# Blockwise attention followed by a channel mix: batches 0 and 1 keep token order in scores, exponentials and value products, and only the sums read the exponentials class by class

## The chip, the core and the metric

One Trainium2 chip, one core of it. The metric is the device time of one execution in microseconds (us). The kernel before took 270.37 us, the median of five executions (268.53 to 272.26). Differences under about one per cent are smaller than the spread of these five.

## What is computed

Two functions follow one another: an attention over 8 batches, 8 heads, 576 tokens and 64 dimensions, with a causal mask by blocks of 64 tokens, and a channel mix over the 4608 tokens by 512 channels that it gives.

```python
scores = scale * np.matmul(q, k.transpose(0, 1, 3, 2))
...
mask = block_i >= block_j
scores = np.where(mask, scores, -1000000000.0)
scores = scores - np.max(scores, axis=-1, keepdims=True)
attn = np.exp(scores)
attn = attn / (np.sum(attn, axis=-1, keepdims=True) + 1e-09)
return np.matmul(attn, v).astype(np.float32)
...
xk = mu_k * x + (1.0 - mu_k) * x_prev
xr = mu_r * x + (1.0 - mu_r) * x_prev
k = np.maximum(xk @ w_k, 0.0)
v = k * k @ w_v
r = 1.0 / (1.0 + np.exp(-(xr @ w_r)))
return (r * v).astype(np.float32)
```

All inputs are float32; the kernel works in bf16 and f16 for the matmul operands and adds up in float32. It takes no maximum before the exponential.

## The kernel before

**Attention.** For a batch, queries and keys of a pair of heads stand in `qkt` as 64 rows a head (the dimension) by 576 tokens. Batches 0 and 1 (`TURNED = 2`, line 21) get there by transposes on TensorE (`add_turned`, line 444) and lie in the order of the tokens. The six later batches are loaded so that one partition holds four tokens running, are transposed by a DMA (`add_qk`, line 509), and their first 512 tokens lie by class: first all tokens whose number is 0 modulo 4, then those with 1, and so on, 128 of each.

A **score** task (`add_score`, line 630; named s, batch, pair, number) multiplies a tile of 128 keys with a stretch of queries, for the two heads of a pair at once: each head uses 64 of the array's rows, and their two matmuls run side by side. Three such tasks cover a pair, and a fourth for each half batch the last 64 tokens (s, batch, t, half). Line 666 is the matmul over the first 512 tokens: a pair streams 1280 columns through it (batch 0: 384, 512 and 384 in its three tasks; the others: 512, 384 and 384), the two heads side by side. It writes PSUM by class for every batch. In the later batches a class is a run of neighbours. In batches 0 and 1 it is every fourth token, so the streamed operand is read with a step of four bf16 elements (8 bytes).

ScalarE takes the exponential of a task's scores in one instruction into `t_e` in f16 (line 695), and VectorE or GpSimd zeroes the masked corner of a diagonal tile (`zero`, line 702).

A **sum** group (`group` and `sums`, lines 747 to 808; tasks d and e) adds the exponentials over the keys. Its stationary operand is 32 columns of `FOURTH`, one of every four of which is one; class by class, a round of four matmuls, one for each of four heads, runs side by side in four groups of 32 array columns. So the sum of class j lands in partition j modulo 4, and 128 columns of PSUM hold 512 tokens. VectorE takes the reciprocal (line 796) and spreads each class over the partitions with a shuffle (line 805): `t_rd` holds the reciprocals by class. A half batch has 1280 columns of class sums for each of the four heads in batches 1 to 7; in batch 0 they are split into a group d with 384 and a group e with 896.

A **value** task (`part` and `value`, lines 762 and 810; tasks v) multiplies the exponentials with the values, again in four column groups, into PSUM by class. VectorE multiplies this with the reciprocals (`norm`, lines 841, 852 and 854) and writes `t_xt` in token order. In that product both inputs are read by class, with a step, and the output runs on.

**Channel mix.** It works on chunks of 512 tokens, the first one in two halves: the difference to the token before (line 930), two scaled additions (line 944), then TensorE tasks k (line 968), r (line 1007) and p (line 1038), with relu, square, tanh and the last product between them on ScalarE, VectorE and GpSimd.

**Order.** Nothing runs in the order in which the program text names it. `Plan` (line 92) holds every task with its engine, a planned duration, what it depends on and which ring of buffers it takes from. TensorE goes through the list `TENSOR` (line 24) exactly; `WHERE` (line 49) names an engine for each task that may run on more than one. The other engines' queues, SP's with the loads among them, and GpSimd's, follow from due times that the plan works out from the TensorE list and the planned durations. `FILL` tasks (line 1073) are dummy matmuls of 128 columns that the plan puts where TensorE would wait before its first k task.

Of the kernel before, what the change touches and what calls it, by code (L numbers as in the profile page):

```python
# [21 lines left out]


TENSOR = """
q000 q010 q001 q011 s0t0 s000 s010 q021 q031 q030 q020 s012 s030 d00 s0t1 s020
s002 q100 v000 s032 d01 q110 q101 q111 v010 s011 s001 s022 s021 e00 s031 k00
k02 k01 k03 v002 v001 s100 q121 e01 s110 s112 s102 q130 v012 v011 s111 s101
q131 q120 k07 k05 k04 k15 s1t0 s120 s1t1 k16 k10 k11 k14 k12 d10 s130 s132 k06
v101 s131 v100 r00 s121 s122 r10 k17 k13 v102 r11 s200 r01 s202 d11 v110 v111
p00 p01 s201 p10 s2t0 s210 p11 s212 k20 k21 k25 k23 k22 r22 s211 k27 r20 v112  # L30
d20 k24 k26 r23 v200 v201 r21 v202 s220 s222 p21 s221 s230 p20 s231 s232 p23
s2t1 s300 v211 d21 s301 v210 s302 p22 s320 s322 v212 s321 s330 s331 k30 k33
s3t1 s332 r32 k31 s310 s3t0 d31 k35 s312 s311 r30 k36 k34 d30 k32 k37 r31 v300
v311 v302 r33 v312 v301 v310 s400 s401 p30 p31 s402 s4t0 p32 s410 s412 p33
s430 k40 s432 k44 k41 s420 s411 k47 r41 s421 k43 s4t1 k45 s431 s422 d40 r42
k42 k46 r40 r43 v400 v402 d41 v401 v411 v410 s500 s501 p42 p41 v412 s5t0 s510
p43 s530 s511 p40 s502 s512 k50 k53 k56 k54 r53 s531 s532 d50 k52 r52 k55 s520
s522 k51 k57 r51 v502 v500 s5t1 s521 r50 p53 v501 d51 v512 v511 s600 s602 p52
v510 s601 s6t0 p50 s630 s632 p51 s610 s611 k60 k67 k62 s612 s620 r63 r61 k66
r62 s6t1 s622 k64 k65 d60 s621 s631 k63 k61 r60 v600 v601 d61 v602 p60 p62  # L40
s700 s702 v612 v610 v611 s701 p61 s720 s721 p63 s710 s722 k70 k73 s711 s712
k74 k72 s7t0 r73 s730 s7t1 d70 v700 r71 r72 s731 s732 k71 k75 k77 k76 v701 d71
v702 v711 p73 p71 v710 v712 p72 p70 r70 k80 k82 k81 k85 k87 k86 k84 k83 r80
r81 r83 r82 p82 p80 p81 r90 p83 r91 k90 k94 k97 k93 k92 k91 k95 k96 r93 r92
p90 p91 p92 p93b p93a
"""


WHERE = {
    "ACT": "ev001 ev011 ev030 ev100 ev110 ev120 ev131 qk1011 qk1100 qk1101 "  # L50
            "qk1110 qk1111 qk201 qk300 qk310 qk330 qk331 qk401 qk411 qk421 "
            "qk501 qk530 qk531 qk600 qk601 qk621 qk630 re02 re04 re06 re07 re11 "
            "re12 re15 re17 re20 re23 re24 re26 re27 re30 re31 re32 re33 re34 "
            "re35 re40 re43 re44 re46 re50 re51 re54 re57 re61 re63 re64 re66 "
            "re67 re70 re77 re80 re81 re82 re83 re85 re90 re91 re92 re95 re96 "
            "sq02 sq04 sq07 sq11 sq12 sq17 sq20 sq21 sq26 sq27 sq30 sq32 sq34 "
            "sq36 sq40 sq44 sq46 sq50 sq54 sq55 sq57 sq61 sq62 sq63 sq70 sq73 "
            "sq74 sq75 sq76 sq81 sq83 sq85 sq87 sq93 sq96 v02 v04 v11 v12 v14 "
            "v20 v21 v24 v30 v31 v40 v54 v70 wk0 wk1 wk2 wk4 wk5 wr1 wr2 wv0 "
            "wv1 wv2 wv3",  # L60
    "DVE": "d11 d12 d13 d21 d31 d33 d43 d52 d60 d62 d72 d82 d90 d91 d93 ev000 "
            "ev010 ev020 ev021 ev031 ev101 ev111 ev121 ev130 qk0010 qk0101 "
            "qk0110 qk1010 qk211 qk220 qk221 qk231 qk301 qk410 qk431 qk631 "
            "qk700 qk710 qk711 qk720 qk721 re00 re01 re03 re05 re10 re13 re14 "
            "re16 re21 re22 re25 re36 re37 re41 re42 re45 re47 re52 re53 re55 "
            "re56 re60 re62 re65 re71 re72 re73 re74 re75 re76 re84 re86 re87 "
            "re93 re94 re97 sq00 sq03 sq05 sq25 sq31 sq35 sq42 sq45 sq47 sq51 "
            "sq52 sq60 sq64 sq66 sq67 sq71 sq72 sq84 sq92 sq94 sq95 v22 v32 v33 "
            "v34 v42 v44 v50 v52 v60 v71 v72 wk6 wr0 wr3 wv4 wv5 wv6 wv7 z002 "
            "z020 z032 z100 z102 z112 z130 z200 z202 z221 z222 z230 z300 z301 "  # L70
            "z310 z321 z322 z330 z411 z412 z420 z421 z422 z430 z431 z432 z501 "
            "z502 z510 z511 z512 z520 z521 z522 z532 z602 z610 z620 z622 z630 "
            "z631 z632 z710 z730 z731",
    "POOL": "d00 d01 d02 d03 d10 d20 d22 d23 d30 d32 d40 d41 d42 d50 d51 d53 "
            "d61 d63 d70 d71 d73 d80 d81 d83 d92 qk0000 qk0001 qk0011 qk0100 "
            "qk0111 qk1000 qk1001 qk200 qk210 qk230 qk311 qk320 qk321 qk400 "
            "qk420 qk430 qk500 qk510 qk511 qk520 qk521 qk610 qk611 qk620 qk701 "
            "qk730 qk731 sq01 sq06 sq10 sq13 sq14 sq15 sq16 sq22 sq23 sq24 sq33 "
            "sq37 sq41 sq43 sq53 sq56 sq65 sq77 sq80 sq82 sq86 sq90 sq91 sq97 "
            "v00 v01 v03 v10 v13 v23 v41 v43 v51 v53 v61 v62 v63 v64 v73 v74 "  # L80
            "wk3 wk7 z000 z010 z012 z022 z030 z101 z110 z111 z120 z121 z122 "
            "z131 z132 z201 z210 z211 z212 z220 z231 z232 z302 z311 z312 z320 "
            "z331 z332 z400 z401 z402 z410 z500 z530 z531 z600 z601 z611 z612 "
            "z621 z700 z701 z702 z711 z712 z720 z721 z722 z732",
}


# [207 lines left out]
def kernel(  # L295
# [23 lines left out]
    J = 4  # L319
# [246 lines left out]
    def add_v(b):  # L566
        for sc in range(5):
            n = P if sc < 4 else D
            vl = plan.buf("vl")
            t = load(("vl", b, sc), lambda: new("vl", [P, H, D], FP),  # L570
                     lambda d, n=n, sc=sc: [(
                         d[0:n], v[b, :, sc * P:sc * P + n].rearrange(
                             "h p d -> p h d"))],
                     0.0051 * n, 0.0108 * n, takes=[vl])

            def fn(eng, n=n, sc=sc):
                convert(eng, VOs[b % 2][0:n, sc],
                        tiles["vl", b, sc][0:n])
            cast["v", b, sc] = flex(
                f"v{b}{sc}", {"POOL": 0.57, "DVE": 0.38, "ACT": 0.52},  # L580
                fn, [t] + ([cast["v", b - 1, 0]] if b and not sc else []),
                takes=[] if sc else [vo_buf[b]],
                uses=[vl] + ([vo_buf[b]] if sc else []))
# [46 lines left out]
    def add_score(b, pr, i):  # L630
# [23 lines left out]
        def fn():  # L654
# [4 lines left out]
            for p, col, kc, a, z in mms:  # L659
                for h in range(2):  # L660
# [1 line left out]
                    keys, ask = qkt[rows, p, 1], qkt[rows, p, 0]  # L662
                    w = z - a
                    keys = keys[:, kc * P:kc * P + P]
                    if a < M:
                        nc.tensor.matmul(  # L666
                            PS[:, h, col:col + J * w].rearrange(
                                "p (j n) -> p j n", j=J), keys,
                            ask[:, 0:CUT].rearrange(
                                "d (p j) -> d j p" if b < TURNED else  # L670
                                "d (j p) -> d j p", j=J)[:, :, a:z],
                            start=True, stop=True)
                    else:
# [28 lines left out]
        def zero(eng):  # L702
            for col, kc, a, z in pieces(b)[i]:
                if a == kc * 32 and a < M:
                    (nc.vector if eng == "DVE" else nc.gpsimd).memset(  # L705
                        tiles["e", b, pr][D:P, :, i, col:col + J * (
                            z - a)].rearrange(
                            "p h (j n) -> p h j n", j=J)[:, :, :, 0:D // J],
                        0.0)
# [3 lines left out]
                f"z{b}{pr}{i}", {"POOL": 0.19 * n, "DVE": 0.09 * n}, zero, [t],  # L713
                uses=[ebuf], lock=())

    def probs(b, head, kc, a, z):


        if kc == J:
# [5 lines left out]
        E = tiles["e", b, pr][:, h, i, col:]  # L725
        if a == M:
            return E[:, 0:D]
        return E[:, 0:J * (z0 - a0)].rearrange("p (j n) -> p j n", j=J)[
            :, :, a - a0:z - a0]

    def add_values(b, Q):

# [29 lines left out]
        def part(PS, xs, a, z):  # L762
            V = VOs[b % 2]
            wide = J * (z - a) if a < M else D
            for n, x in enumerate(xs):
                cols = slice(n * wide, n * wide + wide)
                kcs = [kc for kc in range(J) if kc * 32 < z] + [J] * (a == M)
                for kc in kcs:
                    lo = max(a, kc * 32)
                    for g in range(G):  # L770
                        ps = PS[:, cols]
                        if a < M:
                            ps = ps.rearrange("q (j n) -> q j n", j=J)[
                                :, :, lo - a:z - a]
                        tiled(ps, V[:, kc, 4 * Q + g, x:D:2],
                              probs(b, 4 * Q + g, kc, lo, z), g,
                              kc == kcs[0], kc == kcs[-1])

        def group(name, a, z, deps, steps, dur, r_dur, s_dur):
# [50 lines left out]
        def scale(t, i, xs, a, z, c, first, lo, hi, buf, rd, spr, key):  # L830
# [5 lines left out]
            def norm():  # L836
# [3 lines left out]
                if a == M:  # L840
# [4 lines left out]
                    return  # L845
                p0, p1 = (lo - b * S) // J, (hi - b * S) // J
                num = num[:, 0:n * J * (z - a)].rearrange(
                    "q (s j p) -> q s p j", s=n, j=J)[:, :, p0 - a:p1 - a]
                r = r[:, 0:J * MP].rearrange("q (j p) -> q p j", j=J)[:, p0:p1]
                x = x.rearrange("q s (p j) -> q s p j", j=J)  # L850
# [12 lines left out]
                xt_of[c].setdefault(2 * Q + x, []).append(n)  # L863

        if b == 0:
            rd = group(f"d0{Q}", 0, H2, after(0), 32, 0.34, 0.5, 0.56)
            value(0, (0, 1), 0, H2, after(0), 16, 0.34, *rd)
            rd = group(f"e0{Q}", H2, M, after(0, 1, 2), 84, 0.75, 0.9, 0.56)
            value(1, (0, 1), H2, M, after(1, 2), 32, 0.78, *rd)
        else:  # L870
            rd = group(f"d{b}{Q}", 0, M, after(0, 1, 2), 84, 0.84, 1.3, 0.82)
            value(0, (0,), 0, M, after(0, 1, 2), 16, 0.56, *rd)
            value(1, (1,), 0, M, after(0, 1, 2), 16, 0.56, *rd)
        value(2, (0, 1), M, WD, after(0, 1, 2) + [ready["l", b, Q]], 40, 0.34,
# [274 lines left out]
```

## Time and profile before

| what | value |
|---|---|
| median of five executions | 270.37 us (268.53 to 272.26) |
| the profiled execution, its own time | 271.18 us |
| span from its first to its last instruction | 269.4 us |
| TensorE matmul busy | 250.6 us, 93%, 4116 matmuls |
| VectorE busy | 228.6 us, 85% |
| ScalarE busy | 183.3 us, 68% |
| GpSimd busy | 108.8 us, 40% |
| DMA | 51.51 MB, mean 191 GB/s |

Each engine has its own row in the profile, with the time in which any of its instructions ran. A matmul's duration includes its way through the array, so matmuls overlap and the row says how much of the time at least one was under way. PE is TensorE, PEld its loads of the stationary operand, DVE VectorE, ACT ScalarE, POOL GpSimd, SP the engine that issues the transfers. In a group line, names stand as written<-read; shapes are partitions by elements.

### The profile page before, as it was taken

The numbers are of one execution on the slowest core, as the hardware profiler recorded it, in microseconds if no ns is written. First come the engines' busy times: TensorE is split into PE (matmuls) and PEld (weight loads), VectorE is DVE, ScalarE is ACT, GpSimd is POOL, SyncE is SP. The second block draws the span as 40 slices with busy tenths as digits, with TensorE's granted clock in tenths as the row PEclk, the third lists the DMA queues.
The fourth block names the chain that finished last, engine by engine and source line by source line (L and its number), as shares of the span: only waits on it lengthen the run. The fifth ranks groups of instructions, "written<-read, shape, count | busy, mean of one in ns | idle before, by whom it ended". The sixth has DMA issues, their size and how long they took to land.

```text
span 269.4 us, 9934 instructions
## 1 busy us (share of the span) xinstructions
PE 250.6 (93%) x4116; PEld 130.1 (48%) x4116; DVE 228.6 (85%) x577; ACT 183.3 (68%) x279; POOL 108.8 (40%) x213
## 2 busy tenths in 40 slices
PE   0798978999998979999999999999999999999995
PEld 0665656454453534544355454544554554444443
DVE  2469989989988696999689998999999999998533
ACT  1479979995767898937983789379736970471250
POOL 3555405634534242554457062236384143340310
PEclk9999979999999989999999999999999999999999
DMA  7999998999999999999999999999999101202204
GB/s 219 299 274 236 299 215 269 199 227 220 235 247 205 185 199 217 289 194 230 225 270 192 202 223 284 143 187 266 259 201 198 59 4 68 93 0 79 80 0 156
DMA packets 118301, 51.51 MB, mean 191 GB/s; under 512 B 102768, under 2 KB 109168, under 8 KB 118256
## 3 DMA queue, kind: packets, MB, share of 16 engines
q1 hardware_dynamic: 118256, 50.88, 86.0%
q8 instruction: 32, 0.52, 0.9%
q14 instruction: 13, 0.11, 0.1%
HBM read 33.56 MB, written 9.44 MB: 160 GB/s over the span
## 4 chain that ended last, share of the span: by engine, by line
PE 72%; DVE 12%; DMA 6%; ACT 6%; issue 2%; POOL 1%; SPq 1%; DVEq 0%; ACTq 0%; POOLq 0%
PE t_mm L968 20%; PE t_mm L1038 18%; PE t_mm L744 11%; PE t_mm L1007 10%; PE t_s L666 7%; ACT t_e L695 4%; DMA t_ld<-in_q_dram 4%; DMA t_qkt<-NB 2%; PE t_s L674 2%; PE t_mm L484 2%; DVE t_xt L852 2%; PE t_mm L1076 1%; DVE t_rd L805 1%; DVE t_k L992 1%; DVE t_o L1050 1%
## 5 line engine op out<-in xcount | busy, mean ns | idle before, releaser
L695 ACT ACTIVATE t_e<-t_s 128x1024 f16<-128x1024 f32 x96 | 94.9, 1027 | 26.9 <-PE t_s L666 15.2
L968 PE MATMUL t_mm<-t_xk,WK 128*128 128x512 f16 (+1 forms) x320 | 69.6, 365 | 0.1
L1038 PE MATMUL t_mm<-WV,t_k 128*128 128x512 f16 (+1 forms) x296 | 66.5, 374 | 0.0
L968 PEld LDWEIGHTS <-WK 128*128 128x128 f16 x320 | 29.7, 99 | 30.1 <-issue 2.9
L1038 PEld LDWEIGHTS <-t_k 128*128 128x128 f16 x296 | 27.2, 98 | 31.3 <-issue 2.0
L992 POOL TENSOR_TENSOR t_k<-t_kr 128x512 f16<-128x512 f32 (+1 forms) x24 | 23.4, 981 | 44.5 <-ACT t_kr L981 25.6
L930 POOL TENSOR_TENSOR t_d<-t_xt 128x512 f32<-128x512 f32 (+1 forms) x25 | 25.9, 1038 | 31.6 <-DVE t_xt L852 26.6
L666 PE MATMUL t_s<-t_qkt 64*128 64x128 bf16 (+3 forms) x272 | 35.1, 327 | 3.6 <-ACT t_e L695 3.2
L1018 ACT ACTIVATE t_t<-t_mm 128x512 f32<-128x512 f32 x36 | 21.4, 602 | 22.6 <-PE t_mm L1007 22.5
L1007 PE MATMUL t_mm<-WR,t_xr 128*128 128x512 f16 x144 | 35.9, 380 | 0.0
L705 POOL MEMSET t_e<- 64x128 f16 x65 | 12.5, 209 | 50.3 <-ACT t_e L695 45.3
L852 DVE TENSOR_TENSOR t_xt<-t_mm,t_rd 128x448 f32<-128x448 f32 (+6 forms) x56 | 30.6, 595 | 1.3 <-PE t_mm L744 1.2
L1050 DVE SCALAR_TENSOR_TENSOR t_o<-t_t,t_mm 128x512 f32<-128x512 f32 (+1 forms) x37 | 24.3, 666 | 8.5 <-PE t_mm L1038 8.3
L981 ACT ACTIVATE t_kr<-t_mm 128x512 f32<-128x512 f32 (+1 forms) x44 | 24.5, 563 | 8.1 <-PE t_mm L968 7.1
L744 PE MATMUL t_mm<-t_e,VO 128*32 128x64 f16 (+4 forms) x1056 | 29.2, 251 | 0.6 <-DVE t_kr L983 0.5
L944 DVE SCALAR_TENSOR_TENSOR t_xk<-t_d,MUK,t_xt 128x512 f16<-128x512 f32 (+1 forms) x40 | 28.9, 748 | 0.2
L944 DVE SCALAR_TENSOR_TENSOR t_xr<-t_d,MUR,t_xt 128x512 f16<-128x512 f32 (+1 forms) x40 | 28.4, 735 | 0.0
L674 PE MATMUL t_s<-t_qkt 64*128 64x64 bf16 x320 | 24.4, 198 | 2.4 <-ACT t_e L695 1.6
L983 DVE TENSOR_SCALAR t_kr<-t_mm 128x512 f32<-128x512 f32 (+1 forms) x36 | 21.9, 623 | 4.0 <-PE t_mm L968 3.8
L744 PEld LDWEIGHTS <-VO 128*32 128x32 f16 x1184 | 19.1, 97 | 12.4 <-issue 7.2
L990 ACT ACTIVATE t_k<-t_kr 128x512 f16<-128x512 f32 (+1 forms) x35 | 20.7, 601 | 2.0 <-DVE t_kr L983 1.5
L674 PEld LDWEIGHTS <-t_qkt 64*128 64x128 bf16 x320 | 14.5, 98 | 14.8 <-issue 11.6
(61 smaller groups left out, 289.7 us busy)
## 6 DMA issues: line engine op xcount, KB each, us to landing
out_dram<-t_o SPq DMA_DIRECT2D x35, 256.0 KB, 3.8
t_vl<-in_v_dram SPq DMA_DIRECT2D x32, 256.0 KB, 5.1
t_ld<-in_k_dram SPq DMA_DIRECT2D x48, 128.0 KB, 4.1
t_ld<-in_q_dram SPq DMA_DIRECT2D x24, 256.0 KB, 4.1
t_ld<-in_q_dram SPq DMA_DIRECT2D x8, 288.0 KB, 5.9
t_ld<-in_k_dram SPq DMA_DIRECT2D x8, 288.0 KB, 4.5
t_ld<-in_moe_w_k_dram SPq DMA_DIRECT2D x8, 256.0 KB, 4.9
t_ld<-in_moe_w_v_dram SPq DMA_DIRECT2D x8, 256.0 KB, 4.2
```

The costliest lines, as they stand in the source:

```text
L666: nc.tensor.matmul(PS[:, h, col:col + J * w].rearrange("p (j n) -> p j n", j=J), keys, ask[:, 0:CUT].rearrange("d (p j) -> d j p" if b < T ...
L674: nc.tensor.matmul(PS[:, h, col:col + D], keys, ask[:, CUT:S], start=True, stop=True)
L695: nc.scalar.activation(tiles["e", b, pr][:, :, i, 0:used], tiles["ps", b, pr, i][:, :, 0:used], AF.Exp, scale=ISQ)
L744: nc.tensor.matmul(ps[g * R:g * R + R], lhs, e, start=start, stop=stop, tile_position=(0, g * R))
L852: nc.vector.tensor_tensor(x[:, 0], num[:, 0], r, ALU.mult)
L930: e.tensor_tensor(d[:, 0:w], x[:, cc, o + 1:o + w + 1], x[:, cc, o:o + w], ALU.subtract)
L944: nc.vector.scalar_tensor_tensor(tiles[name, h][:, cc, o:o + w], tiles["d", c, cc][:, 0:w], (MUK1, MUR1)[n][:, cc:cc + 1], xt_tile(c)[:, c ...
L968: nc.tensor.matmul(ps[:, 0:w], WK[:, cc, jc * P:(jc + 1) * P], tiles["xk", h][:, cc, o:o + w], start=(cc == 0), stop=(cc == CCn - 1))
L992: (nc.vector if eng == "DVE" else nc.gpsimd).tensor_tensor(K2, KR, KR, ALU.mult)
L1007: nc.tensor.matmul(ps, tiles["xr", h][:, cc, o + jt * P:o + (jt + 1) * P], WR[:, cc], start=(cc == 0), stop=(cc == CCn - 1))
L1038: nc.tensor.matmul(ps[:, 0:w], tiles["k2", h][:, jc, off:off + P], WV[:, jc, cols], start=(jc == 0), stop=(jc == JCn - 1))
L1050: nc.vector.scalar_tensor_tensor(tiles["o", c, jt, part][:, 0:w], tiles["t", c, jt][:, cols], 1.0, tiles["pv", c, jt, part][:, 0:w], ALU.a ...
```

## The change

In batches 0 and 1 queries stay in token order. The score matmul streams `ask[:, J*a:J*z]`, a run of neighbours, and writes PSUM in the same order. The exponential is unchanged, and its result is then in token order. The masked corner is one run of 64 columns in place of 16 columns in each of four classes. The value products read the exponentials as one run and write PSUM as one run. The sums go on class by class, and so they now read every fourth f16 element of the exponentials (8 bytes apart). The product with the reciprocals reads PSUM as one run; the reciprocals it still reads by class. Batches 2 to 7 keep their code.

Four planned durations change: those of the sum groups of batches 0 and 1, and that of one conversion of values on VectorE. With them `TENSOR` and `WHERE` are replaced by a new order and a new assignment for the whole kernel; neither is shown here in full. TensorE issues the same matmuls less six of the dummies. Counted over the whole program, VectorE has 3 conversions of w_v and 6 relus fewer, and 5 squares and 2 differences more; ScalarE 6 conversions for q and k more and 8 squares of 512 fewer; GpSimd 3 conversions of w_v, 3 of w_r and 5 squares of 512 more, and 5 conversions for q and k fewer.

```diff
 TENSOR = """
-q000 q010 q001 q011 s0t0 s000 s010 q021 q031 q030 q020 s012 s030 d00 s0t1 s020
-s002 q100 v000 s032 d01 q110 q101 q111 v010 s011 s001 s022 s021 e00 s031 k00
+q000 q010 q011 q001 q020 q030 s000 s010 q021 s002 s012 q031 s030 s032 v000 d00
+q110 s020 q100 s011 s0t0 s001 d01 s021 s031 v010 e00 s0t1 s022 q111 q101 v002
...
             cast["v", b, sc] = flex(
-                f"v{b}{sc}", {"POOL": 0.57, "DVE": 0.38, "ACT": 0.52},
+                f"v{b}{sc}", {"POOL": 0.57, "DVE": 0.38 if sc < 4 else 1.0,
+                              "ACT": 0.52},
...
-                    if a < M:
+                    if a < M and b < TURNED:
+                        nc.tensor.matmul(PS[:, h, col:col + J * w], keys,
+                                         ask[:, J * a:J * z], start=True,
+                                         stop=True)
+                    elif a < M:
                         nc.tensor.matmul(
                             PS[:, h, col:col + J * w].rearrange(
                                 "p (j n) -> p j n", j=J), keys,
                             ask[:, 0:CUT].rearrange(
-                                "d (p j) -> d j p" if b < TURNED else
                                 "d (j p) -> d j p", j=J)[:, :, a:z],
                             start=True, stop=True)
...
                     (nc.vector if eng == "DVE" else nc.gpsimd).memset(
+                        tiles["e", b, pr][D:P, :, i, col:col + D]
+                        if b < TURNED else
                         tiles["e", b, pr][D:P, :, i, col:col + J * (
...
-    def probs(b, head, kc, a, z):
+    def probs(b, head, kc, a, z, flat=False):
...
-        return E[:, 0:J * (z0 - a0)].rearrange("p (j n) -> p j n", j=J)[
-            :, :, a - a0:z - a0]
+        E = E[:, 0:J * (z0 - a0)]
+        if b < TURNED and flat:
+            return E[:, J * (a - a0):J * (z - a0)]
+        return E.rearrange("p (n j) -> p j n" if b < TURNED else
+                           "p (j n) -> p j n", j=J)[:, :, a - a0:z - a0]
...
-                        if a < M:
+                        if a < M and b < TURNED:
+                            ps = ps[:, J * (lo - a):J * (z - a)]
+                        elif a < M:
                             ps = ps.rearrange("q (j n) -> q j n", j=J)[
                                 :, :, lo - a:z - a]
                         tiled(ps, V[:, kc, 4 * Q + g, x:D:2],
-                              probs(b, 4 * Q + g, kc, lo, z), g,
+                              probs(b, 4 * Q + g, kc, lo, z, True), g,
...
                 num = num[:, 0:n * J * (z - a)].rearrange(
+                    "q (s p j) -> q s p j" if b < TURNED else
                     "q (s j p) -> q s p j", s=n, j=J)[:, :, p0 - a:p1 - a]
...
-            rd = group(f"d0{Q}", 0, H2, after(0), 32, 0.34, 0.5, 0.56)
+            rd = group(f"d0{Q}", 0, H2, after(0), 32, 0.48, 0.5, 0.56)
-            rd = group(f"e0{Q}", H2, M, after(0, 1, 2), 84, 0.75, 0.9, 0.56)
+            rd = group(f"e0{Q}", H2, M, after(0, 1, 2), 84, 1.08, 0.9, 0.56)
-            rd = group(f"d{b}{Q}", 0, M, after(0, 1, 2), 84, 0.84, 1.3, 0.82)
+            rd = group(f"d{b}{Q}", 0, M, after(0, 1, 2), 84,
+                       1.2 if b < TURNED else 0.84, 1.3, 0.82)
```

## The prediction

> **What bounds the kernel now.** I read the page first: PE is under way in 93% of the span, and the chain that ended last runs through PE for 72% of it, with 7% in the score matmuls (L666) and 11% in sums and values (L744).
>
> ```profile
> span 269.4 us, 9934 instructions
> PE 250.6 (93%) x4116; PEld 130.1 (48%) x4116; DVE 228.6 (85%) x577; ACT 183.3 (68%) x279; POOL 108.8 (40%) x213
> PE 72%; DVE 12%; DMA 6%; ACT 6%; issue 2%; POOL 1%; SPq 1%; DVEq 0%; ACTq 0%; POOLq 0%
> ```
>
> Batches 0 and 1 are at work up to about 60 us, so I then asked for each engine's busy time by stretch (columns: busy us and count of PE, PEld, DVE, ACT, POOL, then granted clock, DMA share, GB/s).
>
> ```profile
> 20.00:33.70 13.70, 12.24 (x390) 7.91 (x389) 13.36 (x42) 13.54 (x21) 6.63 (x12) 1.00 1.00 268
> 33.70:37.10 3.40, 1.54 (x65) 1.09 (x68) 2.96 (x15) 3.40 (x5) 0.31 (x2) 1.00 0.86 202
> 37.10:40.50 3.40, 3.40 (x69) 2.48 (x57) 2.90 (x7) 1.64 (x4) 0.00 (x0) 0.50 0.95 228
> 45.00:60.00 15.00, 15.00 (x356) 8.35 (x355) 13.66 (x35) 15.00 (x29) 8.78 (x19) 1.00 1.10 212
> 140.00:235.00 95.00, 94.07 (x1670) 47.33 (x1669) 92.47 (x231) 60.70 (x88) 40.03 (x75) 1.00 0.86 172
> ```
>
> The reader is to see three stages. From 20 to 37 us ACT is full (16.94 of 17.10 us) and PE is not (13.78). From 45 us PE is full. From 140 us DVE, 92.47 of 95, is nearly as full as PE. Of PE's waits from 20 to 62 us, 2.2 us were for ACT, 1.2 for nothing that the profile shows, 0.5 for DVE:
>
> ```profile
> PE t_s L666 <- ACT t_e L695: 2.2, 4, 0.7
> PE t_mm L484 <- issue: 1.2, 1, 1.2
> PE t_mm L744 <- DVE t_kr L983: 0.5, 1, 0.5
> ```
>
> **A, the scores read a run.** The same matmuls exist in both forms. First group: 43 to 54.5 us, batch 1, step of four. Second: from 62 us, later batches, a run.
>
> ```profile
> L666 PE MATMUL t_s<-t_qkt 64*128 64x512 bf16 x4 | 1.2, 607 | 0.7 <-ACT t_e L695 0.7
> L666 PE MATMUL t_s<-t_qkt 64*128 64x256 bf16 x4 | 0.8, 394 | 0.0
> ...
> L666 PE MATMUL t_s<-t_qkt 64*128 64x512 bf16 x46 | 8.9, 384 | 0.9 <-ACT t_e L695 0.5 <-DMA t_qkt<-NB 0.4
> L666 PE MATMUL t_s<-t_qkt 64*128 64x256 bf16 x46 | 6.3, 273 | 0.5 <-ACT t_e L695 0.5
> ```
>
> The gain is 607-384 = 223 ns for 512 columns and 394-273 = 121 for 256, about 0.44 ns a column; with the step a column costs (607-394)/256 = 0.83 ns. The eight pairs stream 8 x 1280 = 10,240 columns, which would be 4.5 us. Not all of it counts. Before 20 us the array is slow, whatever the clock row shows: the 256-column value matmul, which reads a run, takes 407 ns there against 273 to 275 later, and the score with its step takes 394, as it does later.
>
> ```profile
> L666 PE MATMUL t_s<-t_qkt 64*128 64x256 bf16 x12 | 2.5, 394 | 0.0
> L744 PE MATMUL t_mm<-t_e,VO 128*32 128x256 f16 x8 | 0.7, 407 | 0.0
> ```
>
> So a score gains nothing there: seven tasks with 7 x 384 = 2688 columns. The two tasks of 384 in the stretch at clock 0.50 gain nothing either. Left are 10,240-2688-768 = 6784 columns by 0.44 = **3.0 us** of PE time.
>
> The Trainium skill's "SBUF — State Buffer", section "Door 1", holds that a step is free while a 16-byte line is hit twice, up to 8 bf16 elements. By that rule A and B would both be 0; the rows show 607 against 384 ns at a step of four, so the measurement decides, and I use it.
>
> **B, the sums read with a step.** No row has a column-tiled matmul reading with a step. In a run, the sum rounds of one half batch show in the timeline as these (start, length):
>
> ```profile
> 20.59 0.39 PE L744 MATMUL t_mm<-t_e,FOURTH 128*32 128x64 f16 x32
> 25.34 0.68 PE L744 MATMUL t_mm<-t_e,FOURTH 128*32 128x64 f16 x64
> 46.09 0.79 PE L744 MATMUL t_mm<-t_e,FOURTH 128*32 128x128 f16 x64
> ```
>
> Less about 0.18 for the last matmul's way out (the 32-column row has 179 ns) these are 0.21, 0.50 and 0.61 us for 384, 896 and 1280 columns in each of four heads. Lower end: 0, if four streams side by side hide the step. Upper end: the four streams of a round take turns, 4 x 0.83 = 3.32 ns a column; two half batches of d1 and e0 and one d0 after 20 us have 2560+1792+384 = 4736 columns, 15.7 us against 1.22+1.00+0.21 = 2.43 now, so 13.3. The nearest row is the score: its two streams run side by side, each at 0.83. I take that for four: 1280 x 0.83 = 1.06 (+0.45 each), 896 x 0.83 = 0.74 (+0.24 each), 384 x 0.83 = 0.32 (+0.11), together **+1.5 us**; the other d0 falls before 20 us.
>
> **What of A and B is on the path.** From 45 to 60 us PE is the bound; there lie five scores, 512+4x384 = 2048 columns, -0.9 us, and both d1 groups, +0.9: nothing. From 20 to 45 us it is -(6784-2048) x 0.44 = -2.1 and +0.6, net -1.5, but ACT sets the pace there, with exponentials of 1.03 us each that a faster score does not shorten; PE would wait longer for ACT in place of computing. Ends: 0 and -1.5. I take a third, **-0.5**, since a score also lies ahead of its own exponential.
>
> **C, the product with the reciprocals.** It reads PSUM as a run, the reciprocals with the step. With both stepped 512 elements take 1052 ns (L854); with both in runs 128 take 276 (L841) where the stepped 128 take 364. Per product of 512 the gain lies between 0 and 4 x 88 = 352 ns; eight products' worth, at most 2.8 us of DVE. Off the path to 45 us, where ACT decides: 0, at best -0.7.
>
> **D, the masked corner** is the same number of zeros in one run: 112 ns on DVE, 209 on POOL now; 0, hidden by POOL's 45.3 us of waiting for ACT before it. The removed dummies (six matmuls) ran only where PE waited: 0.
>
> **E, the new order.** Every queue is drawn anew, so each has steps moved past others. By counts times the rows' means DVE stays within 0.1 us, ACT loses 1.0, and POOL gains 2 to 4 (of that the three w_v conversions, which POOL does not show now, lie between its f16 cast, 608 ns, and its product of 512, 1119). POOL is busy 40%, which covers this on average. On SP the third and fourth loads are now both queries, so the first group's second key load comes one load (0.29 MB, at 230 to 284 GB/s some 1.1 us) later; ACT stands idle 4.2 of 12.6 us from 7.4 to 20 us, which covers it. If that cover is gone, +1.1. What the new order does to PE's 8.3 us of gaps after its start (269.4-250.6, less 7.4 before the first and 3.1 after the last matmul) and to the two stretches of 3.4 us at clock 0.50 (at 37.1 and 98.5 us, each worth up to 1.7) can't be read from this trace. I take 0, between -3 and +4.3 (below).
>
> **Sum.** 269.4-0.5+0+0+0 = 268.9 us of span; with the profiled execution's 1.8 us around it (271.18-269.4) 270.7. That execution is 0.8 above the median of the five, so **269.9** stands against 270.37: no change.
>
> **Rivals.**
> *All of it counts* (faster). The -1.5 is kept whole, and with fewer waits before it the stretch at clock 0.50 at 37 us does not come. For it: PE idled 1.86 of the 3.40 us ahead of that stretch. Against: most of that was 1.2 us of "issue", which the change does not touch. 269.9-1.0-1.7 = 267.2.
> *The new order puts in a stall* (slower). From 80 to 100 us the present order has one: PE is busy 17.39 of 20 us, waits for loads of queries, and then runs 3.4 us at half clock: 2.6+1.7 = 4.3. Another such gives 274.2; it decides above 2.7. For it: the DMA share is 0.86 to 1.3 to past 200 us, and DVE and POOL, which free the load buffers, have changed work. Against: the total work is the same.
> *The four streams take turns* (slower). Then B is up to 13.3 in place of 1.5, and 269.9+11.8 = 281.7; it passes one per cent once B exceeds 1.5+3.2 = 4.7 us, that is (4.7+2.43)/4736 = 1.5 ns a column. Against: two streams show 0.83, and four streams of runs show no turns (1280 columns in 0.61 us).
>
> **How the numbers follow.** A measurement of this kernel tells about one per cent from no change: 267.7 to 273.1. The forecast has 0.50; the faster rival 0.20; the stall 0.23; the turns 0.07. So faster 0.20, same 0.50, slower 0.30. The range takes in the faster rival and the stall with little beyond them, 266.5 to 274.5, and leaves out the turns; for the forecast alone, the ends of A and B's net with C give 268.2 to 270.4, and with half of E's 4.3 above and the one per cent below its own range is 267.7 to 272.5.
>
> **What would show it.** A: the score matmul of 512 columns in batch 1 at about 384 ns. B: the x64 rounds with FOURTH in batch 1 at about 1.25 us in place of 0.79; 0.8 would mean a free step, over 2 turns. The path: PE's wait for ACT before the scores, 2.2 us now, grows if I am right that ACT sets the pace. C: the product of 512 elements in batch 0 below 1052 ns. E: the stretches at clock 0.50, two now, and PE's gaps from 60 to 210 us. The prediction is wrong if those gaps or stretches change by more than the whole of A and B.

## The result and the profile after

| | before | after |
|---|---|---|
| median | 270.27 us (48 runs, 267.56 to 273.63) | 272.72 us (27 runs, 269.59 to 277.46) |
| ratio, 95% interval | | 1.0080 (1.0057 to 1.0104) |
| profiled execution, its span | 271.18, 269.4 us | 272.81, 271.0 us |

The kernel became 0.8% slower, 0.0080 x 270.3 = 2.2 us, with 1.5 to 2.8 us as the interval. The ratio compares the fast runs of the two, those at most 1.5% above the fastest run of their kernel, so it is not the quotient of the two medians. The time lies inside the range of the prediction, but the forecast had summed to -0.5 us, and the interval leaves that out. In what follows, line numbers are those of each kernel: a line of the sums is L744 before, L753 after, L752 or L751 in some experiments.

The page of after, with busy time, clock row and the chain that ended last:

```profile
span 271.0 us, 9939 instructions
...
PE 249.0 (92%) x4110; PEld 132.2 (49%) x4110; DVE 229.5 (85%) x576; ACT 182.8 (67%) x279; POOL 116.8 (43%) x214
...
PEclk9999979999999999999999999999999999999999
...
PE 56%; DVE 19%; DMA 12%; ACT 6%; issue 3%; SPq 2%; POOL 2%; DVEq 0%; POOLq 0%; ACTq 0%
```

PE is under way 1.6 us less than before (249.0 against 250.6), and yet the span is 1.6 us longer. So PE stands still for longer. The chain says the same: PE carries 56% of it in place of 72%, and what PE waits for, DVE and DMA, went from 12% and 6% to 19% and 12%. The same stretches as before, with the columns as before:

```profile
20.00:33.70 13.70, 10.68 (x368) 7.59 (x367) 13.37 (x40) 10.85 (x19) 8.78 (x17) 1.00 0.89 234
...
37.30:40.71 3.41, 3.41 (x52) 2.53 (x45) 3.14 (x7) 3.41 (x6) 1.29 (x3) 0.51 1.16 250
45.00:60.00 15.00, 13.41 (x343) 8.77 (x345) 10.69 (x32) 14.18 (x30) 9.20 (x13) 1.00 1.22 241
60.00:80.00 20.00, 18.58 (x233) 8.75 (x225) 19.05 (x54) 11.94 (x20) 6.27 (x10) 1.00 1.08 233
80.00:100.00 20.00, 18.99 (x344) 9.41 (x343) 18.56 (x45) 16.24 (x21) 10.90 (x20) 1.00 1.15 193
100.00:120.00 20.00, 19.09 (x404) 9.59 (x402) 16.52 (x49) 14.51 (x24) 7.21 (x14) 1.00 1.16 245
```

The kernel before, in the stretches that the prediction did not show:

```profile
60.00:80.00 20.00, 20.00 (x256) 9.06 (x254) 18.50 (x47) 14.04 (x22) 9.01 (x16) 1.00 1.03 226
80.00:100.00 20.00, 17.39 (x313) 8.56 (x312) 16.37 (x40) 16.49 (x21) 8.33 (x19) 0.96 1.20 200
100.00:120.00 20.00, 19.98 (x407) 10.04 (x406) 17.17 (x53) 15.47 (x26) 8.38 (x19) 0.95 1.06 229
```

From 45 to 80 us PE never stood before (15.00 of 15.00, 20.00 of 20.00); now 3.0 us are missing there (1.59 + 1.42). From 80 to 100 us the old order had its own gap of 2.61 us, and the new one has 1.01. So the new order does not add one hole. It moves the holes, and their sum is larger: over 45 to 120 us 4.9 us against 2.6. One stretch at half clock fewer, the one at 98.5 us, gives part of it back. The clock does not carry the loss: the mean granted clock is 0.992 over 28 executions of the changed kernel, and 0.989 to 0.991 over the kernel before in four sets of 28 to 35 that were timed beside the experiments.

PE's waits from 44 us to the end, first after, then before (us in total, times, longest):

```profile
PE t_s L671 <- DMA t_qkt<-NB: 2.6, 2, 1.4
PE t_mm L981 <- DVE t_rd L810: 0.6, 1, 0.6
PE t_mm L981 <- DVE t_xk L957: 0.5, 1, 0.5
PE t_mm L1020 <- DVE t_o L1063: 0.5, 1, 0.5
...
```

```profile
PE t_s L674 <- ACT t_e L695: 1.6, 3, 0.6
PE t_s L666 <- ACT t_e L695: 1.0, 2, 0.5
PE t_mm L744 <- issue: 0.5, 1, 0.5
PE t_s L666 <- DMA t_qkt<-NB: 0.4, 1, 0.4
```

The largest is new: scores of batch 2, at 55.9 and 65.9 us, wait for the DMA transposes of their queries and keys. A second trace of the changed kernel, that of the run after2 below, has both again. The second of them, here and there:

```profile
65.89 0.50 PE L671 MATMUL t_s<-t_qkt 64*128 64x512 bf16 x4 [1.42 <-DMA t_qkt<-NB]
```

```profile
63.79 0.50 PE L671 MATMUL t_s<-t_qkt 64*128 64x512 bf16 x4 [1.42 <-DMA t_qkt<-NB]
```

The span of that second trace is 268.9 us, 2.1 us less, and all of the difference lies ahead of this wait: from there to the end both take 205.1 us (271.0 - 65.89 and 268.9 - 63.79). Two executions of one kernel can thus differ by as much as the change costs, so the 1.6 us between the spans of before and after would by themselves prove no loss. The ratio over many runs shows the loss, and the waits that come again show where to look.

SP's queue shows why the second came late (start, length of the issue):

```profile
49.71 3.53 SPq L387 DMA_DIRECT2D t_vl<-in_v_dram  x2
53.35 2.12 SPq L387 DMA_DIRECT2D t_ld<-in_moe_w_v_dram  x1
55.57 0.93 SPq L387 DMA_DIRECT2D t_ld<-in_k_dram  x2
56.59 0.46 SPq L387 DMA_DIRECT2D t_ld<-in_q_dram  x1
57.14 0.97 SPq L387 DMA_DIRECT2D t_ld<-in_k_dram  x2
58.16 4.21 SPq L548 DMA_TRANSPOSE t_qkt<-NB  x1
```

Its last cast ended on VectorE at 50.8 us (50.22 + 0.56), but the transpose stood behind eight loads and was issued at 58.16, where the kernel before issued it at 55.87.

### The profile page after: what moved, and what is told of

It is laid out like the page before. It is cut to its first block, busy times and chain, and to the rows that moved or that the text cites. A ratio compares the mean times of both kernels' runs of the same rounds, so it can differ in the third digit from the quotient of the medians.

```text
span 271.0 us, 9939 instructions
## 1 busy us (share of the span) xinstructions
PE 249.0 (92%) x4110; PEld 132.2 (49%) x4110; DVE 229.5 (85%) x576; ACT 182.8 (67%) x279; POOL 116.8 (43%) x214
## 4 chain that ended last, share of the span: by engine, by line
PE 56%; DVE 19%; DMA 12%; ACT 6%; issue 3%; SPq 2%; POOL 2%; DVEq 0%; POOLq 0%; ACTq 0%
PE t_mm L981 18%; PE t_mm L1051 14%; PE t_mm L1020 10%; PE t_mm L753 7%; DMA t_qkt<-NB 6%; DMA t_ld<-in_k_dram 4%; PE t_s L671 3%; DVE t_xt L864 3%; DVE t_xr L957 3%; DVE t_xk L957 2%; ACT t_e L699 2%; DMA t_ld<-in_moe_w_k_dram 2%; DVE t_o L1063 2%; SPq L387 2%; PE t_s L678 1%
## 5 line engine op out<-in xcount | busy, mean ns | idle before, releaser
L1005 POOL TENSOR_TENSOR t_k<-t_kr 128x512 f16<-128x512 f32 (+1 forms) x25 | 26.5, 1063 | 29.4 <-DVE t_kr L996 16.6
L994 ACT ACTIVATE t_kr<-t_mm 128x512 f32<-128x512 f32 (+1 forms) x50 | 26.8, 552 | 18.3 <-PE t_mm L981 18.0
L943 POOL TENSOR_TENSOR t_d<-t_xt 128x512 f32<-128x512 f32 (+1 forms) x24 | 23.3, 975 | 33.2 <-DVE t_xt L864 23.8
L957 DVE SCALAR_TENSOR_TENSOR t_xr<-t_d,MUR,t_xt 128x512 f16<-128x512 f32 (+1 forms) x40 | 29.6, 764 | 0.1
L753 PE MATMUL t_mm<-t_e,VO 128*32 128x64 f16 (+4 forms) x1056 | 29.1, 251 | 0.6 <-ACT t_qkt L406 0.5
L671 PE MATMUL t_s<-t_qkt 64*128 64x512 bf16 (+3 forms) x192 | 22.7, 300 | 3.1 <-DMA t_qkt<-NB 2.6
L753 PEld LDWEIGHTS <-VO 128*32 128x32 f16 x1184 | 19.4, 97 | 10.3 <-issue 4.5
L678 PE MATMUL t_s<-t_qkt 64*128 64x64 bf16 x320 | 23.2, 197 | 0.4 <-ACT t_e L699 0.4
L1005 DVE TENSOR_TENSOR t_k<-t_kr 128x512 f16<-128x512 f32 (+1 forms) x26 | 20.0, 776 | 4.2 <-ACT t_kr L994 3.9
L1020 PEld LDWEIGHTS <-t_xr 128*128 128x128 f16 x144 | 13.4, 98 | 17.2 <-issue 2.3
L996 DVE TENSOR_SCALAR t_kr<-t_mm 128x512 f32<-128x512 f32 (+1 forms) x30 | 18.9, 636 | 2.9 <-PE t_mm L981 2.3
```

Source lines behind the costliest of these rows:

```text
L671: nc.tensor.matmul(PS[:, h, col:col + J * w].rearrange("p (j n) -> p j n", j=J), keys, ask[:, 0:CUT].rearrange("d (j p) -> d j p", j=J)[:, ...
L678: nc.tensor.matmul(PS[:, h, col:col + D], keys, ask[:, CUT:S], start=True, stop=True)
L753: nc.tensor.matmul(ps[g * R:g * R + R], lhs, e, start=start, stop=stop, tile_position=(0, g * R))
L957: nc.vector.scalar_tensor_tensor(tiles[name, h][:, cc, o:o + w], tiles["d", c, cc][:, 0:w], (MUK1, MUR1)[n][:, cc:cc + 1], xt_tile(c)[:, c ...
L994: nc.scalar.activation(dst, src, AF.Relu)
L1005: (nc.vector if eng == "DVE" else nc.gpsimd).tensor_tensor(K2, KR, KR, ALU.mult)
```

## The experiments

The theory, **O**: the code is worth about nothing on the path, and the new order costs the 2.2 us. Its rival: the code itself costs it, the stepped sums above all. Within O a second question follows. Either a few late steps carry the loss and can be taken out one by one (the chain), or the queues match each other less well all along, and the next late step takes the place of each one removed (the spread, **S**).

**code_alone**: the changed code with the order, the assignment and the planned durations of before.

```diff
 TENSOR = """
-q000 q010 q011 q001 q020 q030 s000 s010 q021 s002 s012 q031 s030 s032 v000 d00
+q000 q010 q001 q011 s0t0 s000 s010 q021 q031 q030 q020 s012 s030 d00 s0t1 s020
...
-            rd = group(f"d0{Q}", 0, H2, after(0), 32, 0.48, 0.5, 0.56)
+            rd = group(f"d0{Q}", 0, H2, after(0), 32, 0.34, 0.5, 0.56)
```

> The changed code of batches 0 and 1 (scores, exponentials, zeroes, values, sums, product) in the order, the engine assignment and the planned durations of before. Theory O (the new order costs the time; the layout itself gives a little): 0.5 us less than before, between 0 and -1.5. Rival L (the layout costs the time, because the sums lose more than the scores gain on the path): about 2 us more than before. By either, the score matmul of 512 columns in batch 1 takes about 384 ns and the rounds of a class sum of batch 1 about 0.5 to 0.6 us more than before.

Measured: 269.33 us, ratio 0.998 (0.9945 to 1.0016).

**order_alone**: the code of before with the order, assignment and planned durations of after; the edit is the reverse of the one above.

> The code of before (scores with a step, sums in runs) in the order, the engine assignment and the planned durations of the changed kernel. Theory O: 2 to 3 us more than before, since the order alone carries the loss. Rival L: within 0.7 us of before. If both parts cost a share, code alone and order alone add up to the whole change, about +2.2 us.

Measured: 272.59 us, ratio 1.0121 (1.0074 to 1.0169), six runs. O stands and its rival falls: the order costs its per cent with the code of before, and the code without the order costs nothing that can be told. Added up the two would give 1.0101 to 1.0142, and the changed kernel has 1.0080. The intervals overlap, so it is open whether the code is worth about 1 us in the new order. PE's wait for the transposes is there as well. One of the two lasts 2.0 us, to 63.2 us, and a stretch at a clock of 0.60 stands right behind it:

```profile
PE t_s L667 <- DMA t_qkt<-NB: 2.6, 2, 2.0
```

```profile
63.20:66.60 3.40, 3.40 (x17) 1.36 (x18) 2.16 (x10) 2.44 (x3) 0.20 (x1) 0.60 1.01 202
```

**scores_alone**: code_alone, but the sums read runs, which are then other tokens.

```diff
-        return E.rearrange("p (n j) -> p j n" if b < TURNED else
-                           "p (j n) -> p j n", j=J)[:, :, a - a0:z - a0]
+        return E.rearrange("p (j n) -> p j n", j=J)[:, :, a - a0:z - a0]
```

> As the code alone in the order of before, but the sums of batches 0 and 1 read runs of the exponentials as before, so that they add up the wrong tokens: the gain of the scores without the price of the sums. Theory O (a score's gain counts only where TensorE is the bound): 0.5 to 2 us less than before. If ScalarE sets the pace wherever the scores lie: within 0.5 us of before. The difference to the code alone is the price of the sums on the path: 1 to 2.2 us if all of it counts.

Measured: 269.07 us, ratio 0.9995 (0.996 to 1.003).

**sums_alone**: the kernel before, with the step in the sums of batches 0 and 1 alone; they then add up other tokens, too.

```diff
-        return E[:, 0:J * (z0 - a0)].rearrange("p (j n) -> p j n", j=J)[
-            :, :, a - a0:z - a0]
+        return E[:, 0:J * (z0 - a0)].rearrange(
+            "p (n j) -> p j n" if b < TURNED and step else
+            "p (j n) -> p j n", j=J)[:, :, a - a0:z - a0]
...
-                              probs(b, 4 * Q + g, kc, lo, z)[:, j], g,
+                              probs(b, 4 * Q + g, kc, lo, z, True)[:, j], g,
```

> The kernel before, but the sums of batches 0 and 1 read every fourth exponential, so that they add up the wrong tokens: the price of the sums without the gain of the scores. If the TensorE time of the sums is all on the path: 1.5 to 2.2 us more than before; if half of it hides behind ScalarE: about 1 us more.

Measured: 269.77 us, ratio 1.0004 (0.997 to 1.0038). Neither part, alone, shows at the end of the kernel, to within the 0.9 us that these intervals tell: not A's faster scores, and not B's slower sums, for which 1 to 2.2 us had been expected. In scores_alone the trace shows where A goes (its first stretch, then PE's largest wait from 20 to 62 us):

```profile
20.00:33.70 13.70, 10.76 (x390) 7.78 (x389) 13.47 (x43) 13.70 (x21) 6.40 (x12) 1.00 0.96 257
```

```profile
PE t_s L666 <- ACT t_e L698: 2.8, 4, 0.9
```

PE does the same 390 matmuls there in 10.76 us in place of 12.24, ACT is full in both (13.70 and 13.54), and PE's wait for ACT has grown from 2.2 to 2.8 us.

**turn_ahead, wv_dve, wv_turn**: the changed kernel, first with the second transpose of batch 2 moved right behind its last cast in SP's queue, then with the three conversions of w_v that the new assignment gives to GpSimd run by VectorE, then with both.

```diff
-    for t in plan.order(TENSOR.split()):
+    todo = plan.order(TENSOR.split())
+    turn = evac["qkt", 2, 1][0]
+    todo.remove(turn)
+    todo.insert(1 + max(todo.index(d) for d in turn["deps"]), turn)
+    for t in todo:
```

```diff
+                if name == "v" and eng == "POOL":
+                    eng = "DVE"
```

> The changed kernel with one transfer moved: the second transpose by DMA of batch 2, which waits in SP's queue behind eight loads (58.2 us in the trace, its data ready at 50.8), is issued right after its last cast. Nothing else moves. Theory T (the late transpose is the largest part of the new order's price): TensorE's wait of 1.4 us at 64.5 us goes, and 1 to 2 us of the 2.2 us between the changed kernel and the one before. Rival S (the price is spread over many small waits): at most 0.5 us, as the next wait takes its place.

> The changed kernel with the three conversions of w_v that the new assignment gives to GpSimd (1541 ns each in its trace) run by VectorE at the same places of the list. Theory W (they hold up the load buffers, and through them SP's queue, the transpose behind it and a difference of the channel mix): 1 to 2 us less than the changed kernel. Theory T alone: the transpose is issued 1 to 2 us earlier, with 0.5 to 1.5 us less. Rival S: within 0.5 us of the changed kernel, as VectorE is nearly full there.

> Both edits on the changed kernel: the transpose of batch 2 ahead and the w_v conversions on VectorE. Theories T and W together: level with the changed code in the order of before, that is 0 to 0.5 per cent under the kernel before. Rival S: still 0.5 to 1 per cent above the kernel before.

Measured: 1.0073 (1.0045 to 1.01), 1.0071 (1.0041 to 1.0101) and 1.0097 (1.0065 to 1.0129). None of the three gives a gain that can be told from after's 1.0080. In turn_ahead the wait at 65 us is gone, and another of the same size has come at 71 us; PE's waits from 44 us on:

```profile
PE t_mm L753 <- DVE t_e L709: 1.6, 2, 1.3
PE t_s L671 <- DMA t_qkt<-NB: 1.1, 1, 1.1
...
```

Now zeroes of the masked corners are late on VectorE. Its timeline shows what held it:

```profile
61.69 0.43 DVE L414 TENSOR_SCALAR WV<-t_ld 128x512 f16<-128x512 f32 x1 [1.38 <-DMA t_ld<-in_moe_w_v_dram]
...
71.15 0.11 DVE L709 MEMSET t_e<- 64x64 uint32 x1
```

VectorE stood 1.38 us before a conversion that waited for its load, and the rest of its queue came behind it. That the zeroes at 71 us were late by this is what the next run tests.

**load_ahead**: turn_ahead, and that load moved ahead of two loads of values.

```diff
+    first = evac["qkt", 2, 0][0]
+    load6 = cast["w", "v", 6]["deps"][0]
+    todo.remove(load6)
+    todo.insert(1 + todo.index(first), load6)
```

> The changed kernel with two edits of SP's queue: the second transpose of batch 2 moved right behind its last cast (as in the run turn_ahead), and the last w_v load moved ahead of two loads of values. turn_ahead, 1.0073 of the kernel before, had lost its wait for the transpose at 65 us, but VectorE then stood 1.38 us before the conversion of that load (wait for the DMA, to 61.7 us), and the matmuls waited 1.3 us at 71 us for zeroes that came late from VectorE. If the three waits are links of one chain that carries the loss, VectorE's stand at 60 us goes, PE's wait at 71 us goes, and the ratio falls by about 1.3/270 = 0.005 to 1.002 to 1.003. If the loss is spread (each engine's queue a little less well matched everywhere, so that the next late thing takes the place of the one taken away), VectorE's stand goes but the ratio stays at 1.006 to 1.010.

Measured: 271.00 us, ratio 1.0048 (1.0017 to 1.0079), between chain and spread. VectorE's stand is gone, and PE's wait for the zeroes is down from 1.6 to 0.8 us in all, the one at 71 us from 1.3 to 0.4; but a transpose is late at 122 us, where it was not before:

```profile
PE t_s L671 <- DMA t_qkt<-NB: 1.2, 1, 1.2
PE t_mm L753 <- DVE t_e L709: 0.8, 2, 0.4
...
```

**load_turn4, load_ahead2, after2**: load_ahead with four loads moved behind the transpose that is late at 122 us; and load_ahead and the changed kernel again, on one chip with it.

```diff
+    turn = evac["qkt", 4, 2][0]
+    late = 0
+    for t in [t for t in todo[:todo.index(turn)] if t.get("eng") == "SP"][-4:]:
+        todo.remove(t)
+        todo.insert(todo.index(turn) + 1 + late, t)
+        late += 1
```

> load_ahead with one more edit of SP's queue: four loads (keys, tails, queries, values) that stand ahead of the transpose of pair 2 of batch 4 are moved behind it. In load_ahead VectorE's stand at 60 us was gone and PE's wait at 71 us was down from 1.3 to 0.4 us, but PE then waited 1.15 us at 122 us for that transpose, which the run before it did not show. If such waits simply add up, taking this one away brings 1.15/270 = 0.004: from 1.0048 to about 1.001. If the next late thing takes its place once more, the ratio stays at 1.004 to 1.007 and another wait of about a microsecond stands after 122 us.

> A second timing of load_ahead (1.0048, interval 1.0017 to 1.0079), beside the changed kernel on one chip. If the two links taken out by then carry part of the loss, it lies below after2 by 0.002 to 0.005; if the loss is spread and only changes its place, the two are the same within 0.002.

> The changed kernel itself, timed again as the measure for the two runs beside it: 1.006 to 1.010 of the kernel before by its first timing.

Measured: load_turn4 1.0044 (1.0003 to 1.0085), load_ahead2 1.0040 (1.0001 to 1.008), after2 1.0076 (1.0031 to 1.0121). In load_turn4 the wait at 122 us is gone. Its trace has others that load_ahead's has not: one at 114.7, one at 125.9, and a third transpose that is late at 177 us:

```profile
114.73 1.90 PE L1051 MATMUL t_mm<-WV,t_k 128*128 128x512 f16 x8 [0.83 <-DVE t_rd L810]
...
125.88 0.23 PE L678 MATMUL t_s<-t_qkt 64*128 64x64 bf16 x4 [0.51 <-ACT t_e L699]
```

```profile
177.20 0.39 PE L671 MATMUL t_s<-t_qkt 64*128 64x512 bf16 x2 [1.04 <-DMA t_qkt<-NB]
```

That these took the place of the wait removed is not shown. The one at 177 us stands in the trace of wv_dve as well, in which no load was moved:

```profile
177.52 0.39 PE L673 MATMUL t_s<-t_qkt 64*128 64x512 bf16 x2 [1.27 <-DMA t_qkt<-NB]
```

Nor is the wait at 122 us always 1.15 us long: in the trace of load_ahead2 it is 0.68. So chain and spread may each hold a part. The first two links gave something: load_ahead lies 0.0032 and 0.0036 below the changed kernel in two timings, about 0.9 of 2.2 us, though the intervals overlap. The third gave nothing that can be told, 1.0044 against 1.0040 beside it; but each of these intervals reaches 0.004 to either side, and the whole wait was worth about as much (1.15/270). The rest of the loss, some 1.1 us by the ratios, has no single place that these runs could name.

**code_casts, code_casts2, code_alone2**: in the old order PE's waits from 85 to 99 us are for ACT's exponentials. code_alone with three of ACT's casts for q and k run by GpSimd, twice, and code_alone again.

```diff
+        run = "POOL" if key in ('qk331', 'qk310', 'qk401') else eng
-        t = plan.add(eng, alts[eng], lambda: fn(eng), deps, takes, uses,
+        t = plan.add(eng, alts[eng], lambda: fn(run), deps, takes, uses,
```

> The changed code in the order of before, with three casts of queries and keys between 84 and 92 us run by GpSimd and not by ScalarE, at the same places of the list. There TensorE waits 1.5 us for exponentials and then runs 3.4 us at clock 0.50. If ScalarE sets the pace there: 1 to 2.5 us less than the changed code in the order of before (267 to 268.5 us). If the keys of the next batch are late by themselves: no change.

> A second timing, in five rounds, of the run code_casts (changed code, order of before, three casts for q and k given from ScalarE to GpSimd), whose interval of 0.9927 to 0.9996 just left out no change. If the gain is real, the ratio is again near 0.996 with an interval below 1, and below that of code_alone2 beside it; if it was chance, both are at 0.998 to 1.000.

> A second timing, in five rounds, of the run code_alone (changed code, order, assignment and planned durations of before), which had 0.998 with an interval of 0.9945 to 1.0016. The forecast's terms for the code alone sum to -0.5 us, 0.998. If the code is worth nothing on the path, 1.000; if the whole of A and B counted, -1.5 us, 0.9945.

Measured: 0.9962 (0.9927 to 0.9996), then 0.9974 (0.994 to 1.0008); code_alone2 1.0021 (0.9987 to 1.0056). This is the best version that was run, 269.0 us in both timings. The gain is about 0.3%, at the edge of what five rounds tell: one of the two intervals leaves out no change, the other does not. It does not come the way it was meant to: PE's waits for exponentials from 80 to 100 us are 1.6 us in the trace of code_casts and 1.5 in that of code_alone. Where it comes from, if it is real, is open. code_alone, 0.998 and 1.0021, is no change.

## Why the prediction failed, step by step

**A, the scores: right.** The stretch of 40 to 58 us in after:

```profile
L667 PE MATMUL t_s<-t_qkt 64*128 64x256 bf16 x6 | 0.8, 274 | 0.0
L667 PE MATMUL t_s<-t_qkt 64*128 64x512 bf16 x4 | 0.8, 382 | 0.0
```

382 and 274 ns, where 384 and 273 were forecast.

**B, the sums: right in kind, 0.6 us too small.** The sums of one half batch in after, answering to the 0.39, 0.68 and 0.79 us shown of before:

```profile
21.54 0.54 PE L753 MATMUL t_mm<-t_e,FOURTH 128*32 128x64 f16 x32
...
23.58 1.05 PE L753 MATMUL t_mm<-t_e,FOURTH 128*32 128x64 f16 x64
...
47.27 1.38 PE L753 MATMUL t_mm<-t_e,FOURTH 128*32 128x128 f16 x64
```

That is +0.15, +0.37 and +0.59 us; with two each of the larger, +2.1 us, against the forecast's +1.5: the term that was mis-sized, though not the one that decided. The step costs 0.59/1280 = 0.46 ns a column beyond the 0.48 that the forecast had from 0.61 us for 1280: 0.94 ns, where the two-stream score's 0.83 was taken. Four streams do not take turns, which would have needed 3.32, and the rival built on it, which decided from 1.5 ns a column, is out.

**What of A and B is on the path: right as far as the runs tell.** -0.5 us is a ratio of 0.998; code_alone gave 0.998 and 1.0021, and nothing at all would fit as well. ACT sets the pace up to 34 us, as argued, and scores_alone shows the wait growing. The rival *All of it counts* needed -1.5 us, 0.9945; that is the lower end of the first interval and outside the second.

**C, the product with the reciprocals: no gain, as taken.** VectorE's four products of 512 elements (batch 0) read PSUM by class before and as a run in code_alone:

```profile
L865 DVE TENSOR_TENSOR t_xt<-t_mm,t_rd 128x512 f32<-128x512 f32 x4 | 4.2, 1044 | 0.0
```

1044 ns (1068 in after) against 1052: the gain of up to 352 ns that was kept as the far end did not come. The reciprocals' step was left in, so what PSUM's step costs by itself is not shown. **D, the corner:** 112 ns on VectorE in both, 203 against 209 on GpSimd; nothing.

**E, the new order: this step failed.** It was put at 0, "between -3 and +4.3", because the total work is the same and because GpSimd at 40% busy "covers this on average". The order alone measured +1.2%, 3.3 us (2.0 to 4.6): a loss inside those ends, and far from the value taken. That the time still fell inside the range is owed to the width of E, and not to a term that was worked out. Three things were wrong in it.

First, a mean of busy time says nothing about a queue. What PE waits for are mostly single steps in the queues of SP and VectorE, the largest late by about a microsecond; from 44 us on none is GpSimd's. GpSimd's total was too small as well: its busy time rose by 8.0 us (by 4.6 in the second trace), where 2 to 4 were put. The count in *The change* leaves out two conversions of w_k and one of values that it gains; for q and k it loses 7 and not 5. Second, on SP only the first group's loads were followed past the steps that they were moved behind. The transposes of the later batches, which stand in the same queue and release the scores, were not. How many loads stood ahead of each could have been read from the order of SP's instructions, without a run. Third, the conversions of w_v on GpSimd were bounded by a cast and a product, 608 to 1119 ns. They took 1541, where VectorE's one takes 364:

```profile
L414 POOL TENSOR_SCALAR WV<-t_ld 128x512 f16<-128x512 f32 x3 | 4.6, 1541 | 0.1
```

```profile
L414 DVE TENSOR_SCALAR WV<-t_ld 128x512 f16<-128x512 f32 x1 | 0.4, 364 | 0.0
```

In wv_dve the three run on VectorE, at 393 ns with its own one, and the time stays. So this size was wrong, but it did not carry the loss.

The rival *The new order puts in a stall* had the side and the engines right, and the wrong shape. It looked for one stall of 4.3 us like the one from 80 to 100 us. In its place came several waits of 0.5 to 1.4 us, and the old stall shrank, which fits a loss of 2.2 us and not 4.3. In order_alone its shape did come, with 2.0 us of wait and a stretch at low clock behind it. The bar of 2.7 us was set too low: from the forecast's 269.9 the step to one per cent above 270.37 is 3.2 us, as the rival of the turns has it.

The prediction's own sign of being wrong did not tell the loss. PE's gaps from 60 to 210 us went from 3.6 to 4.8 us, by less than the net 1.5 us of A and B, and one of the two stretches at half clock went away, which points to a gain. But 1.6 us of the new waiting lie from 45 to 60 us, where the sign did not look.

## To carry to other kernels

When a change brings a new order of all queues with it, price the two apart: the old code in the new order and the new code in the old order are two short runs, and here they told which of the two costs. Before such a run, the order of each queue can be read for one thing: how many steps stand ahead of each transfer that releases the bottleneck, against the queue of before. Do not count on a wait that is taken out to be worth its length: here the removal of two waits of 1.4 and 1.3 us gave back about 0.9 us, and that of a third of 1.15 us nothing that could be told.

## What the runs showed of the hardware that was not expected

- A conversion with a factor from f32 to f16, 128x512, takes 1541 ns on GpSimd, where its plain casts of that size to f16 take 675 to 812 ns in the same trace. VectorE's takes 364 there, and 531 on the mean of four in the kernel before. The Trainium skill's "GPSIMD Engine Reference", section "4.1 Engine selection", calls operations of one input there roughly line-rate. By these rows, which decide here, it is a factor of about 3 to 4 behind VectorE.
- The step of four costs a matmul in four column groups at every width, the narrowest too: in code_alone 212 ns for 32 columns and 280 for 128, in place of 179 and 220.

```profile
L752 PE MATMUL t_mm<-t_e,FOURTH 128*32 128x128 f16 x32 | 2.3, 280 | 0.0
...
L752 PE MATMUL t_mm<-t_e,FOURTH 128*32 128x32 f16 x32 | 1.8, 212 | 0.0
```

- A matmul's stream pays for its step; a VectorE product with a step in both inputs gained nothing when PSUM was read as a run and the reciprocals still with the step: 1052 ns before, 1044 to 1068 with PSUM in a run.
